# Attention by token chunk: exp weights copied to V's layout, attention added into the MLP's PSUM, one evacuation per output tile

## The chip, the cores and the metric

One core of one Trainium2 chip. The metric is device microseconds from the first to the last instruction, plus launch, as the runs give it; the profile's span is about 1.7 us shorter. Executions of one kernel mostly agree within one per cent; the kernel before spreads a little more (175.8 to 179.9 us over all sessions). Ratios are the mean time of one kernel's runs over that of the other's of the same rounds on the same chip, so not quite the ratio of the medians that are quoted.

Terms: TensorE multiplies matrices and adds the results up in PSUM, a memory of several banks; ScalarE and VectorE do the elementwise work and bring results from PSUM to SBUF, the main memory on the core (reading a finished bank out is its evacuation). DMA engines copy data; SP only issues DMAs, in the order of its queue. Engines wait for each other by semaphores. The granted clock is the share of full speed that the profile shows for TensorE, 1.00 being all of it.

## The reference, cut to what matters

S = 2048 tokens, D = 512, 32 heads of 16, F = 1792; everything in bf16.

```python
g = sigmoid((x * gate_w).sum(-1, keepdims=True))
# A: each token attends to 8 tokens, those 0, 2, ..., 14 places back, in 32 heads
a = attention(x, wqkv) @ wo
# B: token-mixing MLP
h = layernorm(x)
u = gelu(einsum("bsd,sf->bdf", h, w1) + b1)
b = transpose(einsum("bdf,fs->bds", u, w2) + b2)
return g * a + (1 - g) * b
```

Of the kernel before, what the change touches and what calls it, by code (L numbers as in the profile page):

```python
# [23 lines left out]
VROW = SC + PAD  # L24
# [3 lines left out]
AV_PRE = 2  # L28
LN3_PRIO = 30
NOUT = 12  # L30
V3Q = "sp"
OUTQ = "sp"
NWARM = 7
NWARM2 = 3
NPV = 3
AV_SLOTS = {0: (0, 1, 2, 3), 1: (0, 2), 2: (0,)}[AV_PRE]

# [40 lines left out]
class _Sched:  # L78
# [14 lines left out]
    def add(self, eng, fn, dur, reads=(), writes=(), deps=(), after=(), prio=0, name="", delay=0.0):  # L93
# [23 lines left out]
        return op  # L117

# [164 lines left out]
def _views(nc, es):  # L283
# [15 lines left out]
    region("WO", 4 * D * 2)  # L299
    region("Q5", 4 * S * 2)  # L300
    region("K5", 4 * KROW * 2)
    region("V5", 4 * KROW * 2)
    region("V3", DH * VROW * 2)
    region("LOG", NW * SC * 4)
    region("ATT", NW * SC * 2)
    region("OUTS", 4 * D * 2)
# [24 lines left out]
def bass_gated_mix__sliding_local_dilated__mixer_token_mlp__prompt_kernel(nc, A_x, A_wqkv, A_wo, B_x, B_w1, B_b1, B_w2, B_b2, gate_w, out, dbg=None):  # L331
    with contextlib.ExitStack() as es:
# [23 lines left out]
               view("V3", BF16, [(S, 4), (1, S)]),  # L356
               view("LOG", BF16, [(S, 4), (1, S)], extra=NW * SC),
               view("XT", BF16, [(S, 4), (1, S)], extra=NFT * D)]
# [4 lines left out]
        PV = [view("Q5", BF16, [(4 * SC, 4), (SC, 4), (1, SC)]),  # L363
              view("K5", BF16, [(4 * SC, 4), (SC, 4), (1, SC)]),
              view("PBUF", BF16, [(4 * SC, 4), (SC, 4), (1, SC)])]
        OT = view("V5", BF16, [(S, 4), (1, S)])
        V3 = view("V3", BF16, [(VROW, DH), (1, VROW)])
        LOG = view("LOG", BF16, [(SC, NW), (1, SC)])
        T1 = view("LOG", BF16, [(D, NST), (1, D)])
        ATT = view("ATT", BF16, [(SC, NW), (1, SC)])  # L370
        OUTS = view("ATT", BF16, [(D, NOUT), (1, D)])
# [5 lines left out]
        X4 = [view("OUTS", BF16, [(SC, 2), (1, SC)]), view("ATT", BF16, [(SC, 2), (1, SC)])]  # L377
        X2 = [view("OUTS", BF16, [(1, SC)], extra=2 * SC), view("ATT", BF16, [(1, SC)], extra=2 * SC)]
# [4 lines left out]
        RS = view("PBUF", BF16, [(1, SC)], extra=14 * SC)  # L383
# [8 lines left out]
        MV = view("SMALL", FP32, [(2, NST), (1, 2)], extra=so[0]); so[0] += 2 * NST  # L392
        ZR = view("ZR", FP32, [(1, SC)])
        MV_mean = view("SMALL", FP32, [(2, NST)], extra=so[0] - 2 * NST)
        MV_var = view("SMALL", FP32, [(2, NST)], extra=so[0] - 2 * NST + 1)
# [4 lines left out]
        TH = small(NST)  # L400
        G = small(NST)
# [71 lines left out]
        ld_x("sp", 0, 2)  # L473
        l_x2 = ld_x("sp", 2, 2)
# [26 lines left out]
        wov = A_wo.rearrange("(h t g) d -> g h t d", h=NH, t=4, g=4)  # L501
        d_wo = None
        for g in range(4):
            d_wo = sch.dma("sp", mk_dma(psub(WO, 32 * g, 32, 0, [(D, 4), (1, D)]), wov[g]), 32 * 4 * D * 2, ds_wo,
                           writes=["wo%d" % g], after=prev_dma(), name="d_wo%d" % g)
            init_dmas.append(d_wo)
# [49 lines left out]
        for t in range(NST):  # L556
            A("dve", (lambda t_: (lambda e: e.bn_stats(out=ST6[:, t_, :], in_=X[:, t_, :])))(t), 0.7,  # L557
              reads=["x%d" % t], writes=["st6_%d" % t], name="ln1_%d" % t, prio=-10,
              after=e_front if t < 4 else ())
            A("dve", (lambda t_: (lambda e: e.bn_aggr(out=MV[:, t_, :], in_=ST6[:, t_, :])))(t), 0.15,  # L560
              reads=["st6_%d" % t], writes=["mv"], name="ln2_%d" % t, prio=-10)
        A("act", lambda e: e.activation(out=SD, in_=MV_var, func=AF.Sqrt, bias=1e-5, scale=1.0), 1.6,
          reads=["mv"], writes=["sd"], name="ln_sqrt", prio=-30, delay=8.0)
        A("dve", lambda e: e.reciprocal(out=RSTD, in_=SD), 0.2, reads=["sd"], writes=["rstd"], name="ln_rstd", prio=-30)
        A("dve", lambda e: e.scalar_tensor_tensor(out=NMR, in0=MV_mean, scalar=-1.0, in1=RSTD, op0=ALU.mult, op1=ALU.mult),
          0.2, reads=["mv", "rstd"], writes=["nmr"], name="ln_nmr", prio=-30)
# [104 lines left out]
        rnd = 0  # L671
        pb2_readers = []
        QKB = ((0, 1, 2, 3), (0, 1, 4, 3))
        PB4_ALIAS = ["wqkv%d_%d" % (tn, dt) for tn in range(3) for dt in range(4)] + XTALL + ["b1r", "b2r", "gwr", "gwc"]
        held = []
        for wh in range(2):
            for dl in range(4):
                buf = QKB[wh][dl]
                A("dve", f_qkm(wh, dl, buf), 4.38,
                  reads=["q5_%d_%d" % (dl, sb) for sb in range(4)] + ["k5_%d_%d" % (dl, sb) for sb in range(4)] + ["k5pad"],  # L680
                  writes=["pb%d" % buf] + (PB4_ALIAS if buf == 4 else []), name="qkm_%d_%d" % (wh, dl), prio=0)
                rnd += 1

            def f_qk4(e, wh=wh):
                r = [f_qkr(wh, dl, QKB[wh][dl])(e) for dl in range(4)]
                return r + [f_gz(e)] if wh == 0 else r
            qop = A("pe", f_qk4, 4.6 if wh == 0 else 3.7, reads=["pb%d" % b for b in QKB[wh]] + ["rp"] + (XTALL + ["gwc"] if wh == 0 else []),
                    writes=["lg4", "lg5", "lg6", "lg7"] + (["bank3"] if wh == 0 else []), name="qkr_%d" % wh, prio=-100, delay=BURST_DELAY)
            if 2 in QKB[wh]:
                pb2_readers.append(qop)  # L690
            if wh == 0:
                A("dve", lambda e: e.tensor_copy(out=sub(ZR, 0, [(1, 4), (4, 128)]), in_=sub(ps[:, 3, :], 0, [(128, 4), (1, 128)])), 0.7, reads=["bank3"], writes=["zr"], name="z_ev", prio=-50)
                ds_z = sch.dsem("z")
                for sb in range(4):
                    zsrc = psub(ZR, 32 * sb, 1, 0, [(4, 128), (1, 4)])
                    sch.dma("sp", mk_dma(sub(ZC, 4 * sb, [(1, 4)]), zsrc), 2048, ds_z, reads=["zr"], writes=["zc%d" % sb], name="d_z%d" % sb, prio=0)
                A("act", lambda e: e.activation(out=TH, in_=ZC, func=AF.Tanh, scale=0.5), 1.6, reads=["zc%d" % sb for sb in range(4)],
                  writes=["th"], name="g_tanh", prio=0)
                A("dve", lambda e: e.tensor_scalar(out=G, in0=TH, scalar1=0.5, scalar2=0.5, op0=ALU.mult, op1=ALU.add), 0.15,
                  reads=["th"], writes=["g"], name="g_g", prio=0)  # L700
                A("dve", lambda e: e.tensor_scalar(out=OMG, in0=TH, scalar1=-0.5, scalar2=0.5, op0=ALU.mult, op1=ALU.add), 0.15,
                  reads=["th"], writes=["omg"], name="g_omg", prio=0)
                A("dve", lambda e: e.tensor_tensor(out=C2, in0=OMG, in1=B2C, op=ALU.mult), 0.15,
                  reads=["omg", "b2c"], writes=["c2"], name="g_c2", prio=0)
# [20 lines left out]
        for hc in range(2):  # L725
            cs = slice(256 * hc, 256 * hc + 256)
            h = "_%d" % hc
            for hf in range(2):
# [8 lines left out]
            A("act", (lambda e, cs=cs: e.activation(out=ATT[:, :, cs], in_=LOG[:, :, cs], func=AF.Exp)), 1.95,  # L737
              reads=["log0" + h, "log1" + h], writes=["att" + h], name="sm_exp" + h, prio=0)
        for hc in range(2):
# [6 lines left out]
            def f_rcp(e, cs=cs):  # L746
                with nc.allow_low_precision(reason="the softmax denominator is bf16 in the reference"):
                    return e.reciprocal(out=RS[:, cs], in_=M1[:, cs])  # L748

            A("dve", f_rcp, 1.75, reads=["m1" + h], writes=["rs" + h], name="sm_rcp" + h, prio=0)  # L750
            rsb = sub(RS, 256 * hc, [(0, 8), (1, 256)])
            A("dve", (lambda e, cs=cs, rsb=rsb: e.tensor_tensor(out=ATT[:, :, cs], in0=ATT[:, :, cs], in1=rsb, op=ALU.mult)), 1.2,
              reads=["rs" + h], writes=["att" + h], name="sm_nrm" + h, prio=0)

        ds_v3 = sch.dsem("v3")
        d_v3 = None
        for c in range(4):
            for dh_hi in range(4):
                pst = V5.ap[0][0]
                src = bass.AP(V5.tensor, V5.offset + dh_hi * pst + 512 * c, [[4 * pst, 32], [KROW, 4], [1, VROW]])  # L760
                dst = psub(V3, 32 * c, 32, 4 * dh_hi * VROW, [(VROW, 4), (1, VROW)])
                d_v3 = sch.dma(V3Q, mk_dma(dst, src), 32 * 4 * VROW * 2, ds_v3, issue=(1.2 if V3Q == "pool" else 0.65),
                               reads=["v5_%d_%d" % (dl, sb) for dl in range(4) for sb in range(4)] + ["v5pad"],
                               writes=["v3_%d_%d" % (c, dh_hi)], deps=pb2_readers, name="d_v3_%d_%d" % (c, dh_hi))

        def f_avm(t, wh, buf):
            w0 = 4 * wh
            in0 = sub(V3, 4 * t * VROW + PAD - 2 * w0, [(-2, 4), (VROW, 4), (1, SC)])
            in1 = sub(ATT, w0 * SC, [(SC, 4), (0, 4), (1, SC)])
            return lambda e: e.tensor_tensor(out=PV[buf], in0=in0, in1=in1, op=ALU.mult)  # L770

        def f_ws(t, wh, buf):
            def fn(e):
                ins = None
                for ws_ in AV_SLOTS:
                    for c in range(4):
                        for g in range(4):
                            ins = e.matmul(ps[32 * g:32 * g + 32, 4 + c, :],  # L778
# [260 lines left out]
```

## The kernel before: the parts that the change touches

The kernel lists operations with what they read and write; a list scheduler of its own orders them, engine by engine, from estimated durations, and puts in the semaphore waits. The order on each engine is then fixed. Names: `ph2` is x times W1 (224 matmuls), `ph3` is u times W2 (16 output tiles of 128 tokens, 14 matmuls each), `wo` is the output projection (4 matmuls a tile). All weights and copies are issued on one queue, SP's.

Attention times V worked in four rounds `t` over a copy `V3` of V, in a layout of 32 heads by 4 token chunks on the partitions; TensorE summed the window in bursts of 32 small matmuls and brought the result to the layout that `wo` needs:

```python
        def f_avm(t, wh, buf):                      # VectorE: V3 shifted by the window, times ATT
            w0 = 4 * wh
            in0 = sub(V3, 4 * t * VROW + PAD - 2 * w0, [(-2, 4), (VROW, 4), (1, SC)])
            in1 = sub(ATT, w0 * SC, [(SC, 4), (0, 4), (1, SC)])
            return lambda e: e.tensor_tensor(out=PV[buf], in0=in0, in1=in1, op=ALU.mult)

        def f_ws(t, wh, buf):                       # TensorE: the burst, 16 matmuls for each wh
            def fn(e):
                ins = None
                for ws_ in AV_SLOTS:                # (0,)
                    for c in range(4):
                        for g in range(4):
                            ins = e.matmul(ps[32 * g:32 * g + 32, 4 + c, :],
                                           lhsT=psub(IDENT, 32 * c, 32, 32 * c, [(1, 32)]),
                                           rhs=psub(PV[buf], 32 * c, 32, (ws_ * 4 + g) * SC, [(1, SC)]), ...)
                return ins
            return fn
        ...
        for t in range(4):
            for wh in range(2):
                A("dve", f_avm(t, wh, buf), 4.38, ...)
                ...                                 # three sums of 2048 elements on VectorE
                if wh == 1:
                    A("pe", f_two(list(held)), 0.77, ..., writes=["lg4", "lg5", "lg6", "lg7"], name="ws_%d" % t, ...)
            ...                                     # ScalarE copies ps[4..7] to OT[:, t]
        ...
        for i in range(NST):                        # 16 output tiles of 128 tokens
            ...                                     # ph3: 14 matmuls into one of three banks
            A("act", (lambda i_, bank_: (lambda e: e.activation(out=T1[:, i_, :], in_=ps[:, bank_, :], func=AF.Identity,
                                                               scale=col(OMG, i_), bias=col(C2, i_))))(i, bank), 0.8, ...)
            if i % 2 == 1 and j2 + 3 <= 7:
                ld_w2(j2 + 3)
            if i < NST - 1:
                emit_wo(i)      # 4 matmuls into another bank; VectorE: OUTS = G * ps + T1; DMA to out
            else:
                emit_last(i)    # the same in three pieces
```

The first three W2 loads, each 896 KB, reuse old buffers. `pb1` is the name of one old buffer that the first two of them split between them:

```python
        def ld_w2(j2):
            ds = sch.dsem("w2_%d" % j2)
            al = []
            if j2 < 2:
                al = ["pb1"]
            ...
            return sch.dma("sp", mk_dma(W2S[j2 % 3], w2v[:, :, 256 * j2:256 * j2 + 256]), F * 256 * 2, ds,
                           writes=["w2s%d" % (j2 % 3)] + al, after=d_w1[-1:], name="d_w2_%d" % j2)
```

## Time and profile before

| | before |
|---|---|
| median of 4 runs | 177.34 us (177.23 to 179.85) |
| span of the profiled run (a run of 176.69 us, 0.65 below the median) | 175.0 us |
| first projection matmul | 7.02 us |
| last matmul ends | 171.03 us |
| from there to the end | 3.97 us |

The page gives busy time by engine and by slice; the timeline gives, for each run of like instructions, start, length, engine, line, operation, count and, in brackets, the idle time before it and who ended it. TensorE runs almost without a break between the two matmuls in the table; the lines for that are in the prediction below.

### The profile page before, as it was taken

The page shows a single profiled execution, that of the slowest core. Times are in us where ns is not written, and L with a number is a line of the kernel's source. Part 1 is how long each engine was busy: PE and PEld are TensorE (multiplying, and loading weights), DVE is VectorE, ACT ScalarE, POOL GpSimd, SP SyncE. Part 2 cuts the span into 40 slices and gives each one's busy share as a digit, 9 for nine tenths or more (in the row PEclk, how much of TensorE's full clock was granted, in tenths as well). Part 3 has the DMA queues.
Part 4 walks back from the last instruction along what each step waited for, and adds up shares of the span by engine and source line. Part 5 has one row for each costly group of instructions (what it writes and reads, how often), then busy time and mean ns, then how long its engine had stood idle before and what let it go on. Part 6 is the DMA issues. An engine that isn't in the chain of part 4 may idle for free.

```text
span 175.0 us, 2471 instructions
## 1 busy us (share of the span) xinstructions
PE 167.9 (96%) x1011; PEld 80.8 (46%) x1029; DVE 145.8 (83%) x147; ACT 77.0 (44%) x103; POOL 0.9 (0%) x8
## 2 busy tenths in 40 slices
PE   7899999999999999999999999999999999999990
PEld 3775555455444444444444443444444444444450
DVE  0787449999979998099799999999999999818853
ACT  2276666966277431399713115313613523160010
POOL 1000000000000000000000000000000000000000
PEclk9999999999999999999999999999999999999999
DMA  5999999950002699998299900075276250003432
GB/s 149 324 237 237 167 277 238 285 131 4 0 1 60 121 154 263 154 229 229 57 308 290 230 0 0 0 210 160 59 204 189 83 151 0 0 0 135 157 131 60
DMA packets 44990, 24.87 MB, mean 142 GB/s; under 512 B 8116, under 2 KB 44980, under 8 KB 44980
## 3 DMA queue, kind: packets, MB, share of 16 engines
q1 hardware_dynamic: 44980, 24.72, 58.7%
q8 instruction: 8, 0.13, 0.3%
q14 instruction: 2, 0.02, 0.0%
HBM read 18.88 MB, written 2.10 MB: 120 GB/s over the span
## 4 chain that ended last, share of the span: by engine, by line
PE 76%; DVE 13%; ACT 6%; issue 3%; DVEq 0%; POOL 0%; POOLq 0%
PE ps L870 28%; PE ps L584 20%; PE ps L831 9%; PE ps L887 7%; DVE arena L770 5%; PE ps L666 4%; ACT arena L737 2%; PE ps L607 2%; PE ps L519 2%; PE ps L778 1%; DVE arena L723 1%; DVE arena L804 1%; DVE arena L797 1%; DVE arena L800 1%; DVE arena L748 1%
## 5 line engine op out<-in xcount | busy, mean ns | idle before, releaser
L870 PE MATMUL ps<-arena 128*128 128x512 bf16 x218 | 48.9, 379 | 0.3
L831 PE MATMUL ps<-arena 128*128 128x512 bf16 x219 | 48.2, 379 | 0.4 <-issue 0.2
L584 PE MATMUL ps<-arena 128*128 128x512 bf16 x171 | 38.1, 379 | 0.5 <-issue 0.2
L659 DVE TENSOR_TENSOR arena<-arena 128x8192 bf16<-128x8192 bf16 x8 | 35.0, 4412 | 2.2 <-ACT arena L595 2.2
L770 DVE TENSOR_TENSOR arena<-arena 128x8192 bf16<-128x8192 bf16 x8 | 35.0, 4416 | 0.0
L831 PEld LDWEIGHTS ps<-arena 128*128 128x128 bf16 x224 | 21.9, 98 | 26.6 <-issue 0.4
L870 PEld LDWEIGHTS ps<-arena 128*128 128x128 bf16 x224 | 21.6, 98 | 27.0 <-issue 1.2
L934 ACT ACTIVATE arena<-ps,arena 128x512 bf16<-128x512 f32 x16 | 12.4, 778 | 43.1 <-PE ps L870 43.1
L584 PEld LDWEIGHTS ps<-arena 128*128 128x128 bf16 x176 | 19.7, 113 | 18.3 <-ACT arena L595 0.6
L595 ACT ACTIVATE arena<-ps 128x512 bf16<-128x512 f32 x32 | 19.0, 598 | 7.1 <-PE ps L584 6.9
L844 ACT ACTIVATE arena<-ps,arena 128x512 bf16<-128x512 f32 x14 | 9.6, 688 | 21.0 <-PE ps L831 20.8
L920 DVE SCALAR_TENSOR_TENSOR arena<-ps,arena 128x512 bf16<-128x512 f32 x15 | 11.3, 750 | 7.3 <-remote 4.2
L887 PE MATMUL ps<-arena 128*128 128x512 bf16 x58 | 13.2, 379 | 0.1
L557 DVE BATCH_NORM_STATS2 arena<-arena 128x6 f32<-128x512 bf16 x16 | 9.9, 681 | 4.0 <-DMA arena<-in_A_x_dram 4.0
L797 DVE TENSOR_TENSOR arena<-arena 128x2048 bf16<-128x2048 bf16 x8 | 9.7, 1216 | 0.0
L800 DVE TENSOR_TENSOR arena<-arena 128x2048 bf16<-128x2048 bf16 x8 | 9.7, 1215 | 0.0
L804 DVE TENSOR_TENSOR arena<-arena 128x2048 bf16<-128x2048 bf16 x8 | 9.4, 1215 | 0.0
L723 DVE TENSOR_TENSOR arena<-arena 128x256 bf16<-128x256 bf16 (+4 forms) x16 | 8.0, 507 | 1.4 <-ACT arena L737 1.0
L887 PEld LDWEIGHTS ps<-arena 128*128 128x128 bf16 x60 | 5.9, 98 | 7.1
L592 ACT ACTIVATE arena<-ps 128x512 bf16<-128x512 f32 x12 | 7.2, 596 | 2.8 <-PE ps L584 2.8
L818 ACT ACTIVATE arena<-ps 128x512 bf16<-128x512 f32 (+1 forms) x7 | 8.0, 1142 | 0.3 <-PE ps L778 0.2
L708 ACT ACTIVATE arena<-ps 128x1024 bf16<-128x1024 f32 x4 | 4.0, 1021 | 8.5 <-PE ps L666 4.6
(56 smaller groups left out, 74.0 us busy)
## 6 DMA issues: line engine op xcount, KB each, us to landing
arena<-in_B_w_dram SPq DMA_DIRECT2D x7, 1024.0 KB, 8.0
arena<-in_B_w_dram SPq DMA_DIRECT2D x8, 896.0 KB, 5.6
arena<-arena SPq DMA_DIRECT2D x16, 131.5 KB, 4.7
out_dram<-arena SPq DMA_DIRECT2D x15, 128.0 KB, 1.7
arena<-in_A_wqkv_dram SPq DMA_DIRECT2D x3, 512.0 KB, 5.1
arena<-in_A_x_dram SPq DMA_DIRECT2D x3, 512.0 KB, 5.7
arena<-in_A_x_dram SPq DMA_DIRECT2D x2, 256.0 KB, 3.0
arena<-in_A_wo_dram SPq DMA_DIRECT2D x4, 128.0 KB, 5.3
```

Of the source, the lines that this page charges most:

```text
L584: ins = e.matmul(ps[:, bank, :], lhsT=lhsT, rhs=XT[:, sb, dt, :], start=(dt == 0), stop=(dt == 3))
L595: return lambda e: e.activation(out=dst, in_=ps[:, bank, :], func=AF.Copy)
L659: return lambda e: e.tensor_tensor(out=PBL[buf], in0=in0, in1=in1, op=ALU.mult)
L770: return lambda e: e.tensor_tensor(out=PV[buf], in0=in0, in1=in1, op=ALU.mult)
L797: A("dve", (lambda b_: (lambda e: e.tensor_tensor(out=PV[b_][:, 0, :, :], in0=PV[b_][:, 0, :, :], in1=PV[b_][:, 1, :, :], op=ALU.add)))(bu ...
L800: A("dve", (lambda b_: (lambda e: e.tensor_tensor(out=PV[b_][:, 2, :, :], in0=PV[b_][:, 2, :, :], in1=PV[b_][:, 3, :, :], op=ALU.add)))(bu ...
L804: A("dve", (lambda b_: (lambda e: e.tensor_tensor(out=PV[b_][:, 0, :, :], in0=PV[b_][:, 0, :, :], in1=PV[b_][:, 2, :, :], op=ALU.add)))(bu ...
L831: ins = e.matmul(ps[:, bank, :], lhsT=W1W[:, slot, st, 128 * e_:128 * e_ + 128], rhs=X[:, st, :], start=(st == 0), stop=(st == NST - 1))
L870: ins = e.matmul(ps[:, bank, :], lhsT=W2S[slot][:, ft, 128 * e_:128 * e_ + 128], rhs=UT[:, ft, :], start=(ft == 0), stop=(ft == NFT - 1))
L887: ins = e.matmul(ps[:, WB(i), :], lhsT=OT[:, t, 128 * i:128 * i + 128], rhs=WO[:, t, :], start=(t == 0), stop=(t == 3))
L920: A("dve", (lambda i_: (lambda e: e.scalar_tensor_tensor(out=OUTS[:, i_ % NOUT, :], in0=ps[:, WB(i_), :], scalar=col(G, i_), in1=T1[:, i_, ...
L934: A("act", (lambda i_, bank_: (lambda e: e.activation(out=T1[:, i_, :], in_=ps[:, bank_, :], func=AF.Identity, scale=col(OMG, i_), bias=co ...
```

## The change

Intent: no summing on TensorE, no second PSUM group and no combine. The exp weights, not V, are copied to the other layout. VectorE makes the output of one token chunk at a time, already normalised by 1/sum and multiplied by exp(z) (z is the gate's logit). As g = (1 - g)·exp(z), `wo` can then add into the PSUM bank of `ph3`, and one ScalarE evacuation with scale 1 - g and bias (1 - g)·b2 ends the tile.

Cut to its core (cuts marked with ...):

```diff
-        ld_x("sp", 0, 2)
-        l_x2 = ld_x("sp", 2, 2)
+        ld_x("sp", 0, 4)
...
+        def ld_er(c, r0, nr, rd, nm):
+            ds = sch.dsem(nm)
+            for g in range(4):
+                src = bass.AP(ATT.tensor, ATT.offset + 32 * c * pst5 + r0 * SC, [[pst5, 32], [1, nr * SC]])
+                dst = bass.AP(ER.tensor, ER.offset + g * pst5 + (c * (NW + 1) + r0) * SC, [[4 * pst5, 32], [1, nr * SC]])
+                sch.dma("sp", mk_dma(dst, src), 32 * nr * SC * 2, ds, reads=rd, writes=["%s_%d" % (nm, g)], deps=er_al, name="d_%s_%d" % (nm, g), prio=-100)
...
+        for wh in range(2):
+            ld_er(0, 4 * wh, 4, ["att_0", "att_1"], ("er0a", "er0b")[wh])
...
+        ld_er(0, NW, 1, ["rs_0", "rs_1"], "er0r")
+        for c in range(1, 4):
+            ld_er(c, 0, NW + 1, ["att_0", "att_1", "rs_0", "rs_1"], "er%d" % c)
...
-        for t in range(4):
+        for c in range(4):
             for wh in range(2):
...
+                P = PP[wh]
+                r_ = ["pp%d" % wh]
+                tt(P, sub(V5, PAD + SC * c - 8 * wh, [(KROW, 4), (-2, 4), (1, SC)]), sub(ER, (c * (NW + 1) + 4 * wh) * SC, [(0, 4), (SC, 4), (1, SC)]),
+                   ALU.mult, 4.4, v_res + er_res(c, wh), r_ + (pp_al[wh] if c == 0 else []), "avm_%d_%d" % (c, wh))
+                ev = sub(P, 0, [(4 * SC, 4), (2 * SC, 2), (1, SC)])
+                tt(ev, ev, sub(P, SC, [(4 * SC, 4), (2 * SC, 2), (1, SC)]), ALU.add, 2.25, [], r_, "ava_%d_%d" % (c, wh))
+                s0 = sub(P, 0, [(4 * SC, 4), (1, SC)])
+                tt(s0, s0, sub(P, 2 * SC, [(4 * SC, 4), (1, SC)]), ALU.add, 1.18, [], r_, "avc_%d_%d" % (c, wh))
+            s0 = sub(PP[0], 0, [(4 * SC, 4), (1, SC)])
+            tt(s0, s0, sub(PP[1], 0, [(4 * SC, 4), (1, SC)]), ALU.add, 1.18, ["pp1"], ["pp0"], "avd_%d" % c)
+            tt(OT[:, :, c * SC:c * SC + SC], s0, sub(ER, (c * (NW + 1) + NW) * SC, [(0, 4), (1, SC)]), ALU.mult, 1.18, ...)
...
-                                   start=(ft == 0), stop=(ft == NFT - 1))
+                                   start=(ft == 0), stop=False)
...
+                    ins = e.matmul(ps[:, bank, :], lhsT=OT[:, t, 128 * i:128 * i + 128], rhs=WO[:, t, :],
+                                   start=False, stop=(t == 3))
...
+        YB = [4, 5, 6, 7, 0, 1, 2]
...
+            A("pe", f_wo(i, bank), 0.865, reads=["ot%d" % (i // 4), "wo"], writes=[br], after=[last_main[0]], name="wo_%d" % i, prio=0)
+            A("act", (lambda e, i=i, bank=bank: e.activation(out=OUTS[:, i, :], in_=ps[:, bank, :], func=AF.Identity,
+                                                             scale=col(OMG, i), bias=col(C2, i))), 0.8, ...)
```

Also in it: the warm-up matmuls go from 7 + 3 to 8 + 1, the QK burst of the second window half is cut in two, layernorm's aggregation is written out, and tanh gives way to exp. A lower `prio` number goes first.

## The prediction

> **What bounds the kernel now.** I read four views of the profile: the page's busy slices, the chain that ended last in order of time, the timelines of VectorE and of TensorE, and the view of the DMA queue's issues. First the slices (each digit is tenths of a 4.4 us slice), and the chain's shares:
>
> ```profile
> PE   7899999999999999999999999999999999999990
> DVE  0787449999979998099799999999999999818853
> ...
> PE 76%; DVE 13%; ACT 6%; issue 3%; DVEq 0%; POOL 0%; POOLq 0%
> ```
>
> TensorE is 90% busy or more in every slice from the third to the last but one. VectorE (83% over the span) has holes, and the chain names it for 13% only because the inferred chain crosses over to whichever engine released an instruction last. What matters is whether TensorE ever waits for VectorE. The TensorE timeline answers that: start, length, what, and in brackets any idle time before it.
>
> ```profile
> 7.02 3.66 PE L607 MATMUL ps<-arena 128*128 128x256 bf16 x32 [0.55 <-DVE arena L557]
> ...
> 73.07 32.75 PE L831 MATMUL ps<-arena 128*128 128x512 bf16 x148 [0.16 <-issue]
> 106.02 0.66 PE L778 MATMUL ps<-arena 32*32 32x512 bf16 x32 [0.20 <-DVE arena L804]
> 106.61 15.28 PE L870 MATMUL ps<-arena 128*128 128x512 bf16 x68
> 121.82 0.65 PE L778 MATMUL ps<-arena 32*32 32x512 bf16 x32
> ```
>
> From 7.02 to 171.03 us TensorE runs without a break worth the name: after 7.02 the brackets add up to about half a microsecond. So the time is the 7.0 us before the first real matmul, plus 164.0 us of TensorE work, plus 4.0 us from the last matmul to the end of the span (175.0). An engine beside TensorE sets the time only if the change makes TensorE wait for it. A cut of TensorE work or of the two ends is worth its full length.
>
> The attention on VectorE before, from its timeline (first of four rounds t):
>
> ```profile
> 90.39 8.76 DVE L770 TENSOR_TENSOR arena<-arena 128x8192 bf16<-128x8192 bf16 x2
> 99.07 1.22 DVE L797 TENSOR_TENSOR arena<-arena 128x2048 bf16<-128x2048 bf16 x1
> 100.21 1.22 DVE L800 TENSOR_TENSOR arena<-arena 128x2048 bf16<-128x2048 bf16 x1
> ...
> 105.88 8.75 DVE L770 TENSOR_TENSOR arena<-arena 128x8192 bf16<-128x8192 bf16 x2
> ```
>
> One round is 105.88 - 90.39 = 15.49 us, and four end at 152.4. All the output projection (L887) needs every round, so TensorE does ph3 first and starts L887 at 155.5: the rounds are hidden already.
>
> **What the Trainium skill says.** (1) "VectorE: DVE Perf Modes", section "The perf-mode tier table": a bf16 tensor_tensor over 2048 elements takes 1224 ns and has no faster mode than two elements a cycle. The trace agrees (1215 ns), so the new products and sums, same operation and type, get no faster per element. (2) "TensorE: Matmul & The Clock Gate", section "Part 3: Packing small matmuls": 16 tiles of 32x32 run side by side. The trace agrees: 32 such matmuls (L778) occupy 0.58 to 0.66 us, though one is listed at 379 ns. So removing 128 of them is worth 2.4 us, not 128 times a matmul. (3) "ScalarE: Activation LUTs", section "What ACT_TABLE_LOAD costs": 1283 ns each. The trace has exactly 1283 ns, eight times; none is in TensorE's way, so removing the one for tanh gives nothing by itself. (4) "Perfetto Trace Analysis", section "Identifying the Most-Contended Engine", warns that matmul busy share is no measure of headroom. That is why I use positions in the timeline and not the 96%.
>
> **The change, part by part.**
> a) *The summing matmuls (L778) go.* On the chain they are 0.66, 0.58, 0.58, 0.58 = 2.40 us. With the first goes its wait (0.20), which also covered the last GELU. The changed ph3 asks only for the first seven UT tiles before its first half (7 matmuls, 1.5 us), and the GELU takes 0.69, so no gap comes back. **-2.6 us.**
> b) *One PSUM group per output tile.* L870 and L887 matmuls remain 224 and 64; adding into an open bank costs no matmul. The last tile's split into 4 + 8 pieces goes: 0.90 becomes 4 x 0.216 = 0.86. **0.0.**
> c) *The end.* Before, after the last matmul (171.03) VectorE still did three serial combines to 172.02, the queue issued the last DMA at 172.38, it landed 1.6 later, the program closed 0.95 after that: 3.97 us. After: one ScalarE evacuation (L934, 778 ns) with 0.04 to start, about 0.05 to the issue, a landing of 1.7 (median of 128 KB outputs, part 6), 0.95 to close: 3.5. **-0.4 us.**
> d) *The front.* x tiles 0 to 3 come in one DMA and not two, so the first weights are issued one issue time (about 0.5 us) earlier. In the queue's own waits the next transfer waited for those weights until 6.90, so they, and not the VectorE line named in the bracket, released the matmul at 7.02. But from 2.5 to 5.5 us the DMA moved 258 to 381 GB/s, about its best rate in this trace: mostly bytes, not issues, set the landing. The longer warm-up (8 x 0.43 against 7) moves the transposes to about 4.7 to 6.4, still ahead. I take **-0.2 us**, anything from 0 to -0.5.
> e) *Second QK burst in two halves.* 64 matmuls still take 3.6 us; one more start costs about the 0.16 shown in a bracket. **+0.15 us**, and the logits come about 1.8 us earlier.
> f) *VectorE by chunk.* By steps in the timeline a product takes 4.34 and a 2048-element sum 1.14. For 4096 elements I interpolate 2.2 (an estimate from these two). A chunk is 2 x 4.34 + 2 x 2.2 + 4 x 1.14 = **17.6 us**, 2.1 more than before; four are 70.6. The normalisation of the weights (2.3) and the combines at the end (12.3) go. None of this is on TensorE's path if the deadlines hold (below). **0.**
> g) *Copies.* V's 16 copies (131.5 KB each, around 50 to 69 us) give way to copies of the exp weights: 8 of 131 KB when the second exp ends, then 4 of 33 KB and 12 of 147 KB. This moves 2.9 MB into the stretch with the last W1 load and three W2 loads. **0 if in time.**
>
> Sum: -2.6 - 0.4 - 0.2 + 0.15 = -3.05; 177.35 - 3.05 = **174.3 us**.
>
> **Deadlines.** In the second exp's place before (ending 83.93), with the logits 1.8 us earlier, it ends near 82. The first four copies need 4 x 0.6 of issue and about 2.5 more to land: first product at about 87, beside the sums and reciprocals that VectorE owes anyway. At worst it starts as before, at 90.4. Chunk ends, early and late: 105/108, 122/126, 140/143, 158/161. On TensorE ph3 begins near 105.6; seven banks let seven ph3 tiles (3.03 us each) run before an output projection must, so the static order should put tile 0's projection near 125, tile 4's near 142, tile 8's near 158, and those of the last chunk last, 4 x 0.87 before the end at about 168, so near 164.5. Smallest margin: 164.5 - 161 = 3.5 us, likely 6. ScalarE evacuates the closing run at 0.78 each against 0.87 per projection: it keeps up.
>
> **Rivals.**
> 1. *A copy wait takes the place of the summing matmuls.* If the weights' copies queue behind W1 and W2 (3.7 MB; before, that burst took 86.5 to 100.2), the first product starts near 100, the last chunk ends near 171 and four projections follow: about 6 us lost, 180. For it: everything goes through one queue and is issued in a fixed order. Against it: the W1 load that heads that burst needs a slot that ph2 frees at about 85.5, the exp ends earlier, and the copies carry the higher priority.
> 2. *The static order puts projections too early.* The order is made from estimated times that leave out table loads; an output projection placed ahead of its OT would stop TensorE in order. For it: before, TensorE did wait at the first L778 (0.20). Against it: a ph3 tile has a longer path behind it than a projection has, so projections should come only when a bank is needed. Each early one would cost 1 to 3 us: 175.5 to 177.
> 3. *The front gives more.* If issue and not bandwidth sets the first weights, -0.5 and not -0.2; with a tail of 3.3, the time is 173.6, over the 2% line (173.8).
> 4. *VectorE becomes the bound.* It would need the last chunk to end over 3.5 us later than my late case. 17.6 per chunk follows from measured steps; only an unseen slower form of the product (strided V, repeated weights) could do it: at one element a cycle, 8 products would each cost 4.3 more and the time pass 195. The product before has a similar form and ran at 4416 ns, so this is unlikely.
>
> **Range and chances.** The summing matmuls (2.6) are nearly certain; the two ends give -0.9 to 0; rivals 1 and 2 give a tail upward of at most one in eight. Hence 174.3, range 172.8 to 176.2. Over 2% faster is under 173.8, half a microsecond below my centre: 0.32. Over 2% slower (above 180.9) needs rival 1 or 4: 0.04. The rest, 0.64, within 2%.
>
> **What would show it.** Right: no 32x32 matmuls; TensorE without idle of over 0.3 us between its first projection and its last matmul, which ends near 168; from there to the end about 3.5; first projection matmul near 6.8; VectorE rounds of about 17.6 with the last ending at 157 to 161; output projections lagging ph3 by about seven tiles. Wrong: brackets before projections that name VectorE or a copy (rivals 1, 2, 4), products much over 4.4 us, a first product after 91, a W2 load landing late before ph3, or a first projection matmul later than 7.0.

## The result, and the profile after

The changed kernel is correct and **slower: 184.3 us** median of 4 runs (183.82 to 185.4), against 177.34 us; ratio 1.037, 95% interval 1.026 to 1.047. It lies above the range.

The slices of the page, after:

```profile
PE   7999999999999999999999993059999999999993
DVE  0755679999799993689999999999999999800000
...
PEclk9999999999999999999999999756999999999999
```

Each digit is now 4.6 us. In the 25th to 27th slice TensorE is at 3, 0 and 5 tenths, where before it had 9 throughout; VectorE is at its full 9 there; and the granted clock falls to 7, 5 and 6 tenths one slice later, in the 26th to 28th. TensorE's timeline has the place (L800 is `ph2`, L839 `ph3`, L848 `wo`):

```profile
70.49 34.71 PE L800 MATMUL ps<-arena 128*128 128x512 bf16 x156
105.03 6.21 PE L839 MATMUL ps<-arena 128*128 128x512 bf16 x28
120.91 16.65 PE L839 MATMUL ps<-arena 128*128 128x512 bf16 x62 [9.67 <-DMA arena<-in_B_w_dram]
137.39 1.03 PE L848 MATMUL ps<-arena 128*128 128x512 bf16 x3
138.25 3.19 PE L839 MATMUL ps<-arena 128*128 128x512 bf16 x14
```

After 28 matmuls, two `ph3` tiles, TensorE stops for 9.67 us until a load of weights lands. In the program the next matmul waits for the second W2 load, and its order explains the rest. SP's timeline shows when the queue issued what (start, length, count):

```profile
79.95 4.97 SPq L439 DMA_DIRECT2D arena<-arena  x8
84.97 5.80 SPq L439 DMA_DIRECT2D arena<-in_B_w_dram  x3
90.81 21.38 SPq L439 DMA_DIRECT2D arena<-arena  x16
112.24 24.20 SPq L439 DMA_DIRECT2D arena<-in_B_w_dram  x4
```

The eight copies of chunk 0 are issued in 4.97 us, 0.62 each on average. Then come three loads: the last of W1, the first and the **third** of W2. Then all 16 remaining copies, in 21.38 us, 1.34 each on average. Only then, at 112.24, the second W2 load is issued. It lands 8.6 us later, at 120.86. The sizes are in part 6 of the page (KB each, median us to landing):

```profile
arena<-arena SPq DMA_DIRECT2D x12, 288.0 KB, 5.8
```

288 KB (295,000 bytes), where the prediction had 147 thousand bytes, 144 in the unit of this row. Other parts of the prediction stand in the profile: no 32x32 matmuls, and the four VectorE rounds in one unbroken run. The first projection matmul starts at 5.93, earlier than the predicted 6.8. The rounds:

```profile
87.57 71.92 DVE L776 TENSOR_TENSOR arena<-arena 128x8192 bf16<-128x8192 bf16 x32
```

It starts at 87.57 (predicted about 87), takes 17.98 a round (17.6) and ends at 159.49 (157 to 161). The time lost is in the stop and in the slow matmuls after it, as the experiments show.

### The profile page after: what moved, and what is told of

Read it like the earlier page. It is cut to its first block, busy times and chain, and to the rows that moved or that the text cites. A ratio compares the mean times of both kernels' runs of the same rounds, so it can differ in the third digit from the quotient of the medians.

```text
span 183.0 us, 2127 instructions
## 1 busy us (share of the span) xinstructions
PE 167.9 (92%) x876; PEld 79.3 (43%) x892; DVE 139.7 (76%) x118; ACT 66.3 (36%) x94; POOL 0.9 (0%) x8
## 4 chain that ended last, share of the span: by engine, by line
PE 68%; SPq 11%; DVE 7%; DMA 7%; ACT 4%; issue 1%
PE ps L839 25%; PE ps L586 19%; SPq L439 11%; PE ps L800 9%; PE ps L848 8%; DMA arena<-in_B_w_dram 5%; PE ps L668 4%; DMA arena<-in_A_wqkv_dram 2%; DVE arena L713 2%; DVE arena L776 2%; PE ps L609 2%; DVE arena L761 2%; ACT arena L727 1%; ACT L727 1%; ACT L564 1%
## 5 line engine op out<-in xcount | busy, mean ns | idle before, releaser
L776 DVE TENSOR_TENSOR arena<-arena 128x2048 bf16<-128x2048 bf16 (+2 forms) x32 | 71.5, 2287 | 0.4
L839 PE MATMUL ps<-arena 128*128 128x512 bf16 x220 | 52.8, 395 | 9.9 <-DMA arena<-in_B_w_dram 9.7
L800 PE MATMUL ps<-arena 128*128 128x512 bf16 x218 | 48.5, 379 | 0.3
L839 PEld LDWEIGHTS ps<-arena 128*128 128x128 bf16 x224 | 22.6, 101 | 38.5 <-DMA arena<-in_B_w_dram 10.2
L586 PE MATMUL ps<-arena 128*128 128x512 bf16 x171 | 38.3, 379 | 0.6 <-issue 0.2
L661 DVE TENSOR_TENSOR arena<-arena 128x8192 bf16<-128x8192 bf16 x8 | 35.0, 4421 | 1.2 <-ACT arena L597 1.2
L800 PEld LDWEIGHTS ps<-arena 128*128 128x128 bf16 x224 | 21.7, 98 | 26.8 <-issue 0.8
L586 PEld LDWEIGHTS ps<-arena 128*128 128x128 bf16 x176 | 19.6, 114 | 18.6 <-ACT arena L597 0.6
L848 PE MATMUL ps<-arena 128*128 128x512 bf16 x63 | 15.4, 379 | 0.1
L848 PEld LDWEIGHTS ps<-arena 128*128 128x128 bf16 x64 | 6.3, 98 | 7.5
L668 PE MATMUL ps<-arena 128*32 128x512 bf16 x128 | 7.5, 380 | 0.0
L570 DVE TENSOR_SCALAR arena<-arena 128x512 bf16<-128x512 bf16 x16 | 5.3, 405 | 0.0
L668 PEld LDWEIGHTS ps<-arena 128*32 128x32 bf16 x128 | 3.1, 96 | 4.1 <-issue 0.4
L513 PE MATMUL ps<-arena 128*128 128x512 bf16 x9 | 3.7, 563 | 1.1 <-POOL arena L426 1.1
L609 PE MATMUL ps<-arena 128*128 128x256 bf16 x32 | 3.7, 273 | 0.2 <-DMA arena<-in_A_wqkv_dram 0.2
```

What stands on the lines that cost most here:

```text
L586: ins = e.matmul(ps[:, bank, :], lhsT=lhsT, rhs=XT[:, sb, dt, :], start=(dt == 0), stop=(dt == 3))
L661: return lambda e: e.tensor_tensor(out=PBL[buf], in0=in0, in1=in1, op=ALU.mult)
L668: ins = e.matmul(ps[32 * c:32 * c + 32, 4 + wl, :], lhsT=RP, rhs=PBL[buf][:, wl, c * 512:(c + 1) * 512], start=(dl == 0), stop=(dl == 3), ...
L776: A("dve", lambda e: e.tensor_tensor(out=o_, in0=a_, in1=b_, op=op_), dur, reads=rd, writes=wr, name=nm)
L800: ins = e.matmul(ps[:, bank, :], lhsT=W1W[:, slot, st, 128 * e_:128 * e_ + 128], rhs=X[:, st, :], start=(st == 0), stop=(st == NST - 1))
L839: ins = e.matmul(ps[:, bank, :], lhsT=W2S[slot][:, ft, 128 * e_:128 * e_ + 128], rhs=UT[:, ft, :], start=(ft == 0), stop=False)
```

## The experiments

Theory Q: the second W2 load lands late because of its place on the one DMA queue, behind 16 copies of 3.67 MB. Rivals: B, the DMA engines cannot move the bytes in time in any order; C, what costs is a dependency of the second W2 load on the first (both are tagged as writers of `pb1`, though they fill different halves); I, what costs is the number of issues. And theory K: a stop makes the matmuls after it slow, and that is lost too. Where the text says that an order is unchanged, the instruction lists of TensorE, VectorE and ScalarE were compared and were the same.

| run | edit | median, us | ratio to before | TensorE's stop in ph3, us |
|---|---|---|---|---|
| changed kernel | | 184.3 | 1.037 | 9.67 |
| e1_w2_free | no false dependency | 177.35 | 1.000 | 3.50 |
| e3_fill | stop filled with matmuls | 181.89 | 1.024 | 9.6 (9.2 of it filled) |
| e5_w2_first | three W2 loads, then copies | 173.45 | 0.976 | 0.68 |
| e6_interleave | queue in the order of need | **171.72** | **0.966** | none |
| e7_half_bytes | copies of 144 KB (wrong result) | 172.32 | 0.975 | none |
| e8_one_copy | one copy for each chunk | 190.93 | 1.081 | 15.09 |
| e11_prio | copies' priority lowered | 176.26 | 0.992 | 2.21 |
| e4_front | before, with the new front | 175.81 | 0.995 | |
| e9_no_burst | before, bursts emptied (wrong result) | 175.49 | 0.993 | |
| e10_split_x | e6 with x in two loads | 173.74 | 0.977 | none |

The runs came from three sessions, on three chips; the kernel before had 177.67 (e1, e3, e5, e6), 177.07 (e4, e7, e8, e9) and 177.53 us (e10, e11). Intervals (95%): e1 0.995 to 1.005, e3 1.020 to 1.028, e5 0.973 to 0.979, e6 0.963 to 0.970, e7 0.970 to 0.979, e8 1.075 to 1.088, e11 0.986 to 0.999, e4 0.990 to 1.001, e9 0.988 to 0.998, e10 0.971 to 0.983. The changed kernel itself was timed in an earlier session (before: 177.34 us) and not again, so each difference to its 184.3 us below compares two sessions; so does e10 with e6.

### e1_w2_free: without the false dependency

```diff
+        pb1_users = sch.users(["pb1"])
         def ld_w2(j2):
-            if j2 < 2:
-                al = ["pb1"]
...
+            ..., deps=(pb1_users if j2 < 2 else ()), ...
```

> The changed kernel with one false dependency taken out: the second W2 load no longer waits for the first one to land (both were tagged as writers of the same old buffer, though they fill different halves). The instruction order of TensorE, VectorE and ScalarE is unchanged; on the one DMA queue the second W2 load now stands ahead of the 16 copies, and the third one takes its place behind them. Theory Q (the 9.7 us stop is the place in the queue: a W2 load stands behind 16 copies of 3.7 MB): the stop moves from the third ph3 tile to the fifth, which TensorE reaches 6 us later, so about 9.7 - 6 = 3.7 us of it are left, the clock falls less, and the time is 175 to 178 us. Rival B (the 16 DMA engines cannot move the bytes in time, in whatever order): the stop stays 9 us or more in sum, 183 us or more. Rival C (the false dependency itself, not the place behind the copies, is what costs): no stop of over 0.5 us at all, 172 us.

```profile
105.03 12.25 PE L839 MATMUL ps<-arena 128*128 128x512 bf16 x56
120.78 9.41 PE L839 MATMUL ps<-arena 128*128 128x512 bf16 x35 [3.50 <-DMA arena<-in_B_w_dram]
```

TensorE's timeline: now 56 matmuls, four tiles, and then a stop of 3.50 us that ends at the same moment as before (120.8). Whichever W2 load stands behind the copies comes then, and TensorE waits for that one. That is what Q said (3.7 us, 175 to 178 us). C is refuted in its pure form: the dependency is gone and a stop is left. Its part was to choose which load fell behind.

### e3_fill: matmuls in the stop

```diff
+            if i == 2:
+                ... f_warm_on(42, bank 3) ...     # 42 matmuls of ones, ahead of the third tile
```

> The changed kernel with 42 matmuls of ones into an unused PSUM bank put into TensorE's order just ahead of the third ph3 tile, where it stops for the W2 load. They take 42 x 0.216 = 9.1 us of the 9.7 us stop and end before the load lands. If the 14 matmuls after the stop ran at half speed because TensorE had been idle (theory K), they now run at full speed and the granted clock stays at 1.0: 3.0 us less, 181.3 us. If the slow stretch comes from the transfer or from the data (rival), they stay slow and the time stays at 184.3 or rises. In both cases the load lands at the same moment, near 121 us from the start of the span.

The views of stretches of the timeline (start:end length, then busy time by engine, granted clock, DMA share, GB/s), changed kernel and then e3:

```profile
113.00:117.00 4.00, 0.00 (x0) 0.00 (x0) 4.00 (x3) 0.00 (x0) 0.00 (x0) 0.94 0.76 179
121.00:123.00 2.00, 2.00 (x5) 0.64 (x6) 1.94 (x2) 0.00 (x0) 0.00 (x0) 0.50 0.78 200
```

```profile
121.00:123.00 2.00, 1.58 (x8) 0.70 (x8) 1.97 (x2) 0.00 (x0) 0.00 (x0) 1.00 0.94 240
```

In the changed kernel the two microseconds after the stop hold 5 matmuls at a clock of 0.50; with the stop filled there are 8 in 1.58 us at 1.00. TensorE's timeline in e3:

```profile
121.56 13.77 PE L840 MATMUL ps<-arena 128*128 128x512 bf16 x63 [0.41 <-DMA arena<-in_B_w_dram]
135.16 1.03 PE L849 MATMUL ps<-arena 128*128 128x512 bf16 x4
```

To size it: from the first matmul after the stop to the first `wo` there are 63 matmuls in both (the changed kernel's trace has records of 62). They took 120.91 to 137.39 = 16.48 us and, filled, 121.56 to 135.16 = 13.60 us. So **2.88 us** of the loss are slow clock and not waiting. Expected 181.3 us, measured 181.9; K holds.

### e5_w2_first and e6_interleave: another order on the queue

Both have e1's edit, and orderings added between DMA issues only (and the scheduler's walk over the operations follows them). `er0r` is the normaliser of chunk 0, `er1` to `er3` are the copies of chunks 1 to 3:

```diff
 # e5: every other copy after the third W2 load
+        for nm in ("er0r", "er1", "er2", "er3"):
+            for o in er_ops[nm]: o.order.add(d_w2[2])
 # e6: W2 0, W2 1, er0r, er1, W2 2, er2, er3
+        for nm in ("er0r", "er1"):
+            for o in er_ops[nm]: o.order.add(d_w2[1])
+        for o in er_ops["er1"]: o.order.update(er_ops["er0r"])
+        d_w2[2].order.update(er_ops["er1"])
+        for nm in ("er2", "er3"):
+            for o in er_ops[nm]: o.order.add(d_w2[2])
```

> The false dependency out, and all three first W2 loads put ahead of the normaliser's and the chunks 1 to 3 copies on the DMA queue; the order on the compute engines is unchanged. Theory Q: TensorE does not stop, 172 us (184.3 less 9.7 of stop and 3.0 of slow clock gives 171.6). VectorE may wait some us for the copies of chunk 1, as 0.9 MB more stands ahead of them, but its last chunk has about 2 us to spare. Rival B (bytes): the stop turns up elsewhere, as VectorE waiting over 4 us for copies and TensorE for its result, 176 us or more.

> The false dependency out, and the DMA queue in the order in which things are needed: first and second W2 load, normaliser and chunk 1 copies, third W2 load, copies of chunks 2 and 3. Order on the compute engines unchanged. Theory Q: neither TensorE nor VectorE waits by more than 0.5 us, 171.6 us, the fastest of the four. Rival B: a wait of several us is left, 176 us or more.

VectorE's timeline in e5 and TensorE's in e6:

```profile
108.60 53.94 DVE L788 TENSOR_TENSOR arena<-arena 128x8192 bf16<-128x8192 bf16 x24 [2.54 <-DMA arena<-arena]
```

```profile
105.09 20.09 PE L859 MATMUL ps<-arena 128*128 128x512 bf16 x91
125.01 1.03 PE L868 MATMUL ps<-arena 128*128 128x512 bf16 x4
```

In e5 the copies of chunk 1 are late by 2.54 us, which VectorE's slack takes, and TensorE stops for 0.68 us for a later W2 load. That is more than expected (no stop, 172 us; measured 173.45); in its profile the first projection matmul is also 0.53 us later than in e6 (6.58 against 6.05). In e6 nobody waits: 91 `ph3` matmuls run through to the first `wo`. It moves the same bytes with the same work on the compute engines and is at **171.72 us** (171.6 expected), 12.6 less than the changed kernel: 9.67 of stop and 2.88 of slow clock make 12.55. Rival B is refuted: the bytes were never too many. **e6 beats both kernels**, by 3.4% the one before.

### e7_half_bytes and e8_one_copy: bytes or issues

```diff
 # e7 (wrong result): rows that were not copied are not read either
-            ld_er(c, 0, NW + 1, [...], "er%d" % c)
+            ld_er(c, 0, 4.5, [...], "er%d" % c)
 # e8: one DMA for each of chunks 1 to 3
+                src = bass.AP(..., [[pst5, 32], [0, 4], [1, nr * SC]])
+                dst = bass.AP(..., [[pst5, 128], [1, nr * SC]])
```

> Wrong result on purpose. The changed kernel, queue order and priorities as they are, with the 12 copies of chunks 1 to 3 cut to 147 KB each, the size that the prediction gave them; they are 288 KB in truth. The products read the rows that are there. If bytes set how long the 16 copies hold the queue (3.67 MB in 21.4 us, 171 KB per us), they now take 1.9 MB / 171 = 11 us, the second W2 load is issued near 102 and lands near 109, before TensorE asks for it at 111.2: no stop over 0.5 us, full clock, 172 us. So with the size as I wrote it the queue order would have done no harm. If the number of issues sets it (16 x 1.34 us), nothing moves: 184 us.

> The changed kernel, queue order and priorities as they are, with one copy of 1.15 MB for each of chunks 1 to 3 (each source row read four times) in place of four of 288 KB: the same bytes, 7 issues in place of 16 ahead of the second W2 load. If bytes set the wait, that load lands at about the same time, near 121, although its issue comes earlier: stop of 8 to 10 us, 183 to 185 us. If the cost of an issue sets it, it lands 8 us or more earlier: a stop under 1.5 us, 172 to 174 us.

SP's timeline in e7; then SP's and TensorE's in e8, and the sizes and landings of its copies:

```profile
91.37 13.05 SPq L439 DMA_DIRECT2D arena<-arena  x16
104.46 19.83 SPq L439 DMA_DIRECT2D arena<-in_B_w_dram  x4
```

```profile
90.71 11.42 SPq L439 DMA_DIRECT2D arena<-arena  x7
102.17 39.61 SPq L439 DMA_DIRECT2D arena<-in_B_w_dram  x4
```

```profile
126.40 16.49 PE L844 MATMUL ps<-arena 128*128 128x512 bf16 x62 [15.09 <-DMA arena<-in_B_w_dram]
```

```profile
arena<-arena SPq DMA_DIRECT2D x3, 1152.0 KB, 23.3
```

With half the bytes and the same 16 issues in the same order, the issues take 13.05 us and not 21.38 (11 expected), the load goes out at 104.46 (102 expected) and TensorE doesn't stop: 172.3 us. So the number of issues is not what counts (rival I falls), and with the size that the prediction used, the harmful order would have done no harm. With 7 issues in place of 16 and the same bytes, the load is issued ten microseconds earlier (102.17) and yet lands **later**, at 126.4, 24 us after its issue. I read both as one: an issue takes long when earlier bytes are still on their way, and a load issued earlier waits behind them all the same. That fits the numbers but is argued, and e8 is not a clean test, as its queue also moved less: 187 GB/s over 90 to 112 us, against 225 in the changed kernel. That e8 would be 6.6 us worse than the changed kernel I did not expect (183 to 185). Its copies read each source row four times and land only after 23.3 us in the median; why, no run here shows.

### e11_prio: the priority alone

```diff
-                sch.dma(..., deps=er_al, name=..., prio=-100)
+                sch.dma(..., deps=er_al, name=..., prio=(-100 if r0 + nr <= NW else 0))
```

> The changed kernel with one number altered: the copies of the normaliser and of chunks 1 to 3 lose their raised priority; the false dependency between the first two W2 loads stays. On the DMA queue the second W2 load now stands behind 11 of the 16 copies in place of all 16; the order of TensorE, VectorE and ScalarE is that of the changed kernel. Theory Q: it is issued near 103.5 in place of 112.2 and lands near 111, about when TensorE asks for it (111.2): a stop of 0 to 1.5 us, no slow clock, 172 to 173.5 us. If the false dependency itself were the cause, the stop of over 9 us would stay: 184 us.

```profile
113.32 15.46 PE L839 MATMUL ps<-arena 128*128 128x512 bf16 x62 [2.21 <-DMA arena<-in_B_w_dram]
```

```profile
113.00:117.00 4.00, 3.68 (x11) 1.47 (x12) 4.00 (x3) 0.00 (x0) 0.00 (x0) 0.64 0.98 229
```

```profile
104.40 1.33 SPq L439 DMA_DIRECT2D arena<-in_B_w_dram  x1
```

TensorE's timeline, a stretch of it, and SP's timeline. With the dependency still in, five copies fewer ahead of the load bring it 7.8 us forward (issued 104.40 against 112.24). So the place among the copies is the cause, and the raised priority gave it that place. A stop of 2.21 us is left, a little over my 0 to 1.5, and the time, 176.3, misses my 172 to 173.5 by far more than that: even this short stop drops the clock (0.64 over the 4 us), and 63 matmuls to the first `wo` take 15.30 us in place of 13.60, another 1.7 lost. I had expected no slow clock here. In shorter stretches the clock is 1.00 from 113 to 114, 0.57 from 114 to 115, 0.50 from 115 to 117 and 0.72 from 117 to 118: it fell when TensorE had already been at work again for most of a microsecond.

### e4_front, e10_split_x and e9_no_burst: the parts that were to save time

```diff
 # e4, in the kernel before
-        ld_x("sp", 0, 2); l_x2 = ld_x("sp", 2, 2); NWARM = 7; NWARM2 = 3
+        ld_x("sp", 0, 4); NWARM = 8; NWARM2 = 1
 # e10, in e6: the reverse, but for the warm-up
-        ld_x("sp", 0, 4)
+        ld_x("sp", 0, 2); ld_x("sp", 2, 2)
 # e9, in the kernel before (wrong result): each burst is two matmuls of 64 columns
-                            ins = e.matmul(ps[32*g:32*g+32, 4 + c, :], ...)     # 32 of them
+                return e.matmul(ps[:, 4, 0:64], lhsT=IDENT, rhs=sub(PV[buf], 0, [(1, 64)]), ...)
```

> The kernel before with the front of the changed one alone: x tiles 0 to 3 in one load, warm-up of 8 + 1 matmuls in place of 7 + 3. The order of TensorE from the first projection on is that of before. The prediction gave this 0.2 us, because bytes were to set when the first weights land. In the changed kernel they landed about 1.1 us earlier, so: first projection matmul near 6.0 (7.02 before), 1.0 us less, 176.5 against 177.5 us. If 0.2 was right and something else in the changed kernel moved the weights: 177.3.

> The mended kernel (DMA queue in the order of need) with x tiles 0 to 3 loaded in two halves again, as before the change; the warm-up stays at 8 + 1 matmuls and every other order is the same. If loading them in one piece is what brought the first weights forward (by about 1.0 us, where the prediction said 0.2), the first projection matmul moves from about 6.05 back to 6.9 or later and the time rises by 0.8 to 1.2 us, to 172.7. If the warm-up numbers or the run did it, the time stays at 171.7. The profile's own wait of the next transfer for the weights tells: 5.9 in one piece, 6.9 in two.

> Wrong result on purpose. The kernel before with each of the four bursts of 32 summing matmuls cut to 2 matmuls of 64 columns, so that the semaphores and waits stay and the work goes (the order of everything else is that of before). The prediction gave the bursts 2.40 us of TensorE's path and 0.20 of wait. Two short matmuls with their start should cost some 0.1 us each time: 2.0 to 2.4 us less, 175.3 us. If the bursts were hidden (by the last GELU, or by VectorE), 177.4.

SP's own wait for the first weights, e10 (x in two loads) and then e6 (in one), and what the DMA engines moved in the fifth microsecond in each (last column, GB/s):

```profile
SPq L469 <- DMA arena<-in_A_wqkv_dram: 4.4, 1, 4.4
```

```profile
4.00:5.00 1.00, 1.00 (x8) 0.70 (x7) 0.00 (x0) 0.00 (x0) 0.00 (x0) 1.00 0.57 171
```

```profile
SPq L469 <- DMA arena<-in_A_wqkv_dram: 3.0, 1, 3.0
```

```profile
4.00:5.00 1.00, 0.64 (x10) 0.42 (x9) 0.00 (x0) 0.00 (x0) 0.00 (x0) 1.00 1.08 385
```

TensorE's first projection, again in e10 and then in e6:

```profile
7.89 3.66 PE L619 MATMUL ps<-arena 128*128 128x256 bf16 x32 [1.10 <-DMA arena<-in_A_wqkv_dram]
```

```profile
6.05 3.66 PE L618 MATMUL ps<-arena 128*128 128x256 bf16 x32 [0.17 <-DMA arena<-in_A_wqkv_dram]
```

e4's first projection matmul starts at 5.98 (before 7.02) and its median is 1.26 us lower (1.0 expected); the interval of the ratio touches 1, as the kernel before had a run of 175.79 in that session. e10 is clearer: with x in two loads the weights land so late that the first projection matmul starts at 7.89 in place of 6.05, and the time rises by 2.0 us, 1.8 by the ratios to before (172.7 us expected). The start varies from run to run: in the profiles with x in two loads it is 7.02 (before), 7.79 (e9) and 7.89 (e10), in the nine with one load 5.86 to 6.65. One load in place of two is worth 1 to 2 us, not 0.2. The rate shows a gap: 171 GB/s in the fifth microsecond with two loads (300 in the kernel before), 385 with one. What makes the gap, no run here shows.

In e9, bursts two to four go from 0.58 to between 0.06 and 0.10, some 1.5 us saved together, near the gain in the median (1.58; 2.0 to 2.4 expected). The first saves nothing, for with its work gone TensorE waits 0.35 us for the last GELU there. The prediction had named that cover; the changed kernel's `ph3` asks only for the first seven UT tiles and so has no such wait.

## Why the prediction was wrong

It said 174.3 us in a range of 172.8 to 176.2; the time was 184.3. By its steps:

| step | predicted, us | measured, us |
|---|---|---|
| a, b, e: TensorE from first projection to last matmul | -2.45 | 164.01 to 161.66 in e6: -2.35 |
| c: the end | -0.4 | 3.97 to 2.89 in e6: -1.08 |
| d: the front | -0.2 | 7.02 to 6.05 in e6: -0.97 |
| f: VectorE, 17.6 a chunk, hidden | 0 | 17.98 a chunk, hidden in e6: 0 |
| **g: the copies, "0 if in time"** | **0** | **+9.67 stop, +2.88 slow clock in the changed kernel** |

1. **Step g failed, in three ways.** The size was wrong: nine rows of 1 KB on 32 partitions are 288 KB, and I wrote half of that. So 4.7 MB went into the stretch and not 2.9; e7 shows that at my size nothing would have stopped. Then I asked the question in one direction only: rival 1 has the copies behind W1 and W2, and I never asked what the copies delay. I had seen in the diff that they carry the higher priority and booked it as an argument *against* a loss; it is the cause of it (e11, e5, e6). The list of signs of being wrong does name "a W2 load landing late before ph3", but no rival and no cost stood behind it, and the 0.04 for over 2% slower was given to rivals 1 and 4, neither of which came. And I did not see that the second W2 load has to wait for the first to land, by the shared name `pb1`; in the kernel before, with no copies about, that cost nothing. e1 shows that this chose the load that suffered.
2. **The estimate inside the kernel was wrong in the same way.** Its scheduler books 0.65 us for an issue and 320 GB/s; running it gives the second W2 load's issue at 97.3 and its landing at 110.6, 1.1 us before its own time for the third tile (111.7). On the chip the issue came at 112.24. The order was "in time" by a margin smaller than the error of its terms.
3. **A term was missing:** the clock. I valued a wait at its length. Here 9.67 us of wait cost 12.55, and in e11 2.21 cost 3.9. Nor does the loss simply grow with the stop. In e1 (stop of 3.50 us) the clock was 0.65 from 120.5 to 122, 0.50 to 124 and 0.82 to 125; if it was either half or full, this makes 3.4 us at half clock, and so do e11's stretches above (stop of 2.21 us). Each lost 1.7 us (e1: 35 matmuls from 120.78 to 130.03 us, 9.25 us, where e3's rate makes it 7.56).
4. **The gains were under-estimated.** With the copies in order (e6) the sum is -4.4 us of span, where I had -3.05. By the medians it is -5.95 us, as the profiled run of before (176.69 us) lies below its median and that of e6 (172.37 us) above; where the remaining 1.5 us are, the two profiles can't show. So e6 at 171.72 us lies below my range (from 172.8): with step g in order I would have missed on the other side. The front: I read a range of 258 to 381 GB/s as "about its best rate" though its low end (258 GB/s, 4.0 to 4.5 us) was in the gap that the change closes (385 GB/s over 4 to 5 us in e6). The end: the last issue comes at 168.53 and the span ends 2.07 later, where before it was 2.6; the queue then waited through a row of output semaphores (six waits from 172.9 on in the profile), and now for one. That these are the difference is argued and not tested. Rival 3's sum has a slip: its own terms give 173.7 to 173.8 us and not 173.6, so at the 2% line and not over it.
5. **What held:** the sum of a, b and e (-2.35 for -2.45; e9 alone isolates 1.5 us of the bursts), VectorE's rounds, the deadline of the first `wo` (predicted near 125, in e6 125.01), and that VectorE's longer work stays hidden. Rivals 2 and 4 did not come; rival 3 did (the front), hidden under the stop. The start of the first product (87.57, predicted about 87) was partly luck: the second exp ended at 79.86 and not near 82, and the product followed straight on VectorE's own sums and reciprocals, not on a copy.

## What to carry to other kernels

When copies are added to a queue that also carries weights, list for each transfer when it is needed, what stands ahead of it in bytes, and at which rate that drains; then ask the question both ways, what delays the new transfers and what they delay. A raised priority is a debt of whatever stands behind. And value a TensorE stop by more than its length: look at the granted clock after it (2.21 us of stop brought a slow clock here, 0.68 us did not).

## What the Trainium skill lacked or had wrong

- "TensorE: Matmul & The Clock Gate", section "HAM oscillation — how this bites in real kernels", gives the rule that TensorE idle gaps must not exceed about 3.4 us. In e11 a gap of 2.21 us was enough: a clock of 0.64 over 113 to 117 us and 1.7 us lost. In e5 a gap of 0.68 us cost nothing more. After 9.67 us of gap 2.88 us were lost.
- "DMA: Bandwidth & Descriptors", section "Issuing engines are not separate DMA queues", calls the time to issue a DMA usually small relative to the DMA. It lacks how far an issue stretches on a queue with transfers outstanding: 0.62 us a copy at first and 1.34 on average behind three loads of 2.9 MB, so that 16 issues held the queue for 21.38 us, and 13.05 us with half the bytes in 12 of them (e7).
- No page read here has a rate for copies between partitions of SBUF from 32 source partitions. A copy of 288 KB landed after 5.8 us in the median; one of 1152 KB that reads each source row four times, after 23.3.
